# A fused attention and hard-swish kernel: first pair's load converted in the transfer, transpositions, staircases and second bias sums moved

## The chip, the cores and the metric

The kernel runs on one core of one Trainium2 chip. The metric is the device time of one execution in microseconds (us), the median of several runs. A core has five engines that run side by side and wait for each other by semaphores. PE (TensorE) does matrix products and transpositions, DVE (VectorE) elementwise work and scans, ACT (ScalarE) exponentials and copies, POOL (GpSimd) further elementwise work, and SP (SyncE) only issues transfers. POOL issues transfers as well, into a queue of its own; the profile calls it the software queue (q0), and that of SP the hardware queue (q1). A transfer that POOL issues can convert f32 to f16 on the way, and in this kernel only POOL's do.

## What is computed

`q, k, v` are 8 batches of 8 heads of 576 positions of 64 numbers, `s` has one number for each head and position. The output is 4608 rows (batch and position) of 512.

```python
scores = q @ k.T / 8
cum = cumsum(max(s, 0))                        # along the positions of a head
scores = where(causal, -1e9, scores + min(-(cum_i - cum_j), 0))
attn = softmax(scores)                         # sum + 1e-9 below
x = (attn @ v), heads side by side             # 4608 x 512
h = x @ w_in                                   # 512 x 2048
out = (h * clip(h + 3, 0, 6) / 6) @ w_out      # 2048 x 512
```

## The kernel before

**Slots.** The 64 heads are taken in 32 pairs. The main loop (line 718) runs over the pairs p, and one pass through it is called slot p here. Slots 0 to 3 hold attention alone. From slot 4 on, pieces of the second half are laid between the pieces of attention: each `group()` (line 533) emits one piece, either `m1` (four 512-column matmuls `ph` on line 452 for one of 16 column blocks of `h`, then ACT's ReLU on line 467 and DVE's product `gT` on line 468) or `m2` (four matmuls `po` on line 479). A hand-written plan (line 506) says which one comes in slots 4 to 13; later the two alternate as their inputs come ready. After the last slot a tail of `group()` calls works off the rest. All engines take their instructions strictly in the order in which this Python text emits them.

**Attention of a pair.** `load_qk(p, i)` loads q (i = 0) or k (i = 1). For pairs 1 to 10 POOL's queue does it and converts to f16, into a tile `tok` with 96 partitions that hold six positions each. For the pairs for which `flat(p)` is true (p = 0, and p from 11 on) SP or ACT load the f32 numbers into `raw`, and `cast_qk` converts them, on ACT for pair 0 and on POOL later. `transpose_in` puts q or k through PE into a PSUM tile `pt`; `transpose_out` copies `pt` into the tile `qk` on DVE or ACT (`order`, line 211, for the flat form; line 251 for the other). From pair 11 on a transposing transfer (`crossbar_qk`, line 266) and DVE's `spread` take PE's place. `scores` (lines 298 to 335) makes three score tiles of a head in PSUM, each with an exponential on ACT, `corner` the small rest; the score tiles have two buffers. `av` (line 386) multiplies by v, `norm` (lines 408 and 409, DVE) divides by the row sums and makes `x`. `transpose_x` (PE line 423, DVE copy on line 428) puts `x` into `xT`, the input of `m1`; from pair 7 to pair 30 a transposing transfer on SP's queue, `crossbar_x` (line 436), does that.

**The bias.** `cum1` to `cum6` (lines 637 to 665) take the running sums of `s` for 32 heads at a time and split them into rows that the score matmuls can add up. Pair 0 reads them through `pick`. For all later pairs `load_aug` (line 143) copies four rows for each head into partitions 64 to 67 of `qk`; it needs finished rows, and partitions 64 to 127 that nobody writes afterwards. The first 32 heads are done ahead of the loop by DVE and ACT. The second 32, needed from pair 16 on, are done between slots 9 and 13, by POOL except for the scan (line 645), which is DVE's.

**Staircases.** From pair 8 on the causal mask comes from constant staircases in partitions 68 to 127 of `qk`. `set_stair` (line 594) copies them once into each of the four `qk` buffers, a copy for each head: on POOL in slots 6 and 7, on ACT in slots 8 and 9, both heads in one go at the slot's top. `load_aug(p + 2)` has to come behind it, since the copy covers its four partitions too.

**Queues that matter for the change.** ACT's order at the start is: loads, `spos`, `rows_of` (line 690), the two casts of pair 0 (line 183), the two copies of q (line 211). DVE's is: sums (lines 645 to 665), `pick(0)` (line 668), the two copies of k, `pick(1)`. SP's is: `s`, q of pair 0, v of pair 0, then `load_aug(1)` (line 143), which waits for the finished rows, and behind it v of pair 1. POOL's is: constants, q and k of pairs 1 and 2, `cast_v(0)`, q and k of pair 3, `cast_v(1)`, which waits for v of pair 1, and then a long row of loads that ends with the weights `w_in` and `w_out`.

Of the kernel before, what the change touches and what calls it, by code (L numbers as in the profile page):

```python
# [18 lines left out]
def kernel(  # L19
# [10 lines left out]
    nc = tc.nc  # L30
# [7 lines left out]
    NP = NHEADS // 2  # L38
# [5 lines left out]
    NPE = 2 * PPB + 3  # L44
# [4 lines left out]
    NVRAW = 2  # L49
    VW = 66  # L50
    NROW = 1
    NWARM = (16, 4)

# [47 lines left out]
    toks = {}  # L103

    def flat(p):
        return p < 1 or p >= NPE

    def load_qk(p, i, eng=nc.sync):
        b, h0 = p // PPB, 2 * (p % PPB)
        src = (q, k)[i][b, h0 : h0 + 2]  # L110
        if not flat(p):
            if not i:
                tok = work.tile([128, 24 * D], F16, tag="tok", bufs=4, name="tok")
                toks[p] = tok[0:96].rearrange("p (i h e d) -> p i h e d", i=2, h=2, e=6)
            nc.gpsimd.dma_start(
                out=toks[p][:, i].rearrange("p h e d -> p h (e d)"),
                in_=src.rearrange("h (p e) d -> p h (e d)", e=6),
            )
        else:
            eng.dma_start(  # L120
                out=raws[p % NRAW].rearrange("p (i t d) -> p i t d", i=2, t=9)[:, i],
                in_=src.rearrange("h s d -> (h s) d").rearrange(
                    "(t p) d -> p t d", p=128
                ),
            )
# [40 lines left out]
    def fill(eng, ap, value):  # L166

        word = np.array([value, value], np.float16).view(np.float32)[0]
        eng.memset(ap.bitcast(F32), float(word))
# [8 lines left out]
    def cast_qk(p, copy=nc.gpsimd.tensor_copy):  # L178
        tok = work.tile([128, 24 * D], F16, tag="tok", bufs=4, name="tok")
        toks[p] = tok[:, 0 : 18 * D]  # L180
        for i in range(2):
            c = slice(9 * D * i, 9 * D * (i + 1))
            copy(out=toks[p][:, c], in_=raws[p % NRAW][:, c])  # L183
# [373 lines left out]
    def load_s(n, engs):  # L557
# [3 lines left out]
            eng.dma_start(out=C[n][32 * r : 32 * (r + 1)], in_=heads)  # L561

    load_s(0, (nc.sync, nc.scalar, nc.sync, nc.scalar))
    load_qk(0, 0)
    load_qk(0, 1, nc.scalar)
    nc.scalar.preload_act_table_set("natural_log_exp_and_others")
    load_v(0, nc.sync)
    fill(nc.gpsimd, ident, 0.0)
# [6 lines left out]
        base=0,  # L575
        channel_multiplier=-1,
    )
    fill(nc.gpsimd, shut, 0.0)
    for c in (slice(0, 512), slice(512, 640)):
        w = 128 if c.start == 0 else 64  # L580
# [8 lines left out]
            channel_multiplier=-1,  # L589
        )  # L590

    def set_stair(i, copy):
        for hh in range(2):
            copy(
                out=qks[i][64:128, hh, :, 64 * hh : 64 * hh + 640].rearrange(
                    "p i (t c) -> p i t c", c=128
                ),
                in_=stair_sb[64:128, :, None, :].to_broadcast([64, 2, 5, 128]),
            )
# [15 lines left out]
    nc.vector.memset(bias3, 3.0)  # L615
    fill(nc.gpsimd, rows_of[0][:, 0, :], 1.0)
    fill(nc.gpsimd, rows_of[0][:, 1, SEQ:640], 0.0)
    fill(nc.gpsimd, qks[0][64:68, :, :, :], 0.0)
    for i in range(2):
        load_qk(1, i)  # L620
    for i in range(NQK):
# [11 lines left out]
        op=ALU.add,  # L633
    )
    nc.vector.tensor_scalar_mul(out=ident2, in0=ident, scalar1=2.0)

    def cum1(n, eng):
        C["p"] = work.tile([128, SEQ], F32, tag="spos", bufs=1, name="spos")
# [4 lines left out]
    def cum2(n):  # L643
        C["c"] = work.tile([128, SEQ], F32, tag="c8", bufs=1, name="c8")
        nc.vector.tensor_tensor_scan(
            out=C["c"], data0=one.to_broadcast([128, SEQ]), data1=C["p"], initial=0.0, op0=ALU.mult, op1=ALU.add
        )
# [39 lines left out]
        out=C["p"][:, 304:SEQ], in_=C[0][:, 304:SEQ], func=AF.Relu, scale=8.0  # L687
    )
    cum2(0)
    nc.scalar.copy(out=rows_of[0][0:32, 0, 0:SEQ], in_=C["c"][0:32])  # L690
    cast_qk(0, nc.scalar.copy)
    cum3(0, V)
    cum4(0, V)
    cum5(0, V)
    cum6(0, V)
    pick(0)
    transpose(0, 0, (nc.scalar.copy,) * 2)
    transpose(0, 1)
    warm(NWARM[1])
    for g in range(1, 2 * NROW):  # L700
        pick(g)
# [16 lines left out]
    for p in range(NP):  # L718
        nxt = p + 1 < NP
        if NPE <= p + 3 < NP:  # L720
            for i in range(2):
                load_qk(p + 3, i)
        def qk_ahead():
            if PPB < p + 3 < NPE:
                for i in range(2):
                    load_qk(p + 3, i)

        if p == 1:
            load_aug(4, nc.gpsimd)
        elif p == 2:  # L730
            load_w_in(0)
            cast_v(2)
            qk_ahead()
            load_aug(5, nc.gpsimd)
        elif p == 3:
            cast_v(3)
            load_w_in(1)
            qk_ahead()
            load_aug(6, nc.gpsimd)
            cast_v(4)  # L740
        elif p:
            qk_ahead()
            if NPE <= p + 2 < NP:
                cast_qk(p + 2)
                crossbar_qk(p + 2)
            for fn, c in {
                4: ((I, 2),),
                5: ((I, 3),),
                6: ((U, 0), (U, 1), (U, 2), (U, 3)),
                7: ((U, 4), (U, 5), (U, 6), (U, 7)),  # L750
            }.get(p, ()):
                fn(c)
            if nxt:
                cast_v(p + 1)
            if p in (6, 7):
                set_stair((p + 2) % NQK, nc.gpsimd.tensor_copy)
            elif p in (8, 9):
                set_stair((p + 2) % NQK, nc.scalar.copy)
            if p == 4:
                load_aug(7, nc.gpsimd)  # L760
            elif 5 < p < NP - 2:
                load_aug(p + 2, nc.gpsimd)
        if p and p + 2 < NP:
            load_v(p + 2, nc.sync)
        if p == 2:
            nc.sync.dma_start(out=stair_sb, in_=stair_dram.ap())
        if p == 9:
            load_s(1, (nc.sync,) * 4)
            fill(nc.gpsimd, rows_of[1][:, 0, :], 1.0)
        if p == 10:  # L770
            cum1(1, nc.gpsimd)
        if p == 11:
            cum2(1)
            nc.gpsimd.tensor_copy(out=rows_of[1][0:32, 0, 0:SEQ], in_=C["c"][0:32])
        if p == 12:
            cum3(1, nc.gpsimd)
            cum4(1, nc.gpsimd)
        if p == 13:
            cum5(1, nc.gpsimd)
            cum6(1, nc.gpsimd)  # L780

        if p == NPROD + 1:
            x_done[0] = NPROD

        def get(i):
            if p + 1 < NPE:
                transpose(p + 1, i)
            elif nxt:
                spread(p + 1, i)

        if p < PPB:
            scores(p, 0, 0)
            scores(p, 0, 1)
            get(0)
            scores(p, 0, 2)
            corner(p)
            if p:
                av(p - 1, 1, 0)
                av(p - 1, 1, 1)
                norm(p - 1, 1)  # L800
            get(1)
            scores(p, 1, 0)
            scores(p, 1, 1)
            av(p, 0, 0)
            scores(p, 1, 2)
            if p:
                transpose_x(p - 1)
            av(p, 0, 1)
            norm(p, 0)
            continue  # L810

        if p == PPB:
            early[0] = False
            scores(p, 0, 0)
            av(p - 1, 1, 0)
            av(p - 1, 1, 1)
            norm(p - 1, 1)
            m1_begin(0, 0, NKC - 1)
            scores(p, 0, 1)
            transpose_x(p - 1)  # L820
            m1_begin(0, 1, NKC - 1)
            pt = transpose_in(p + 1, 0)
            transpose_out(p + 1, 0, pt, pars=(0,))
            group()
            transpose_out(p + 1, 0, pt, pars=(1,))
            scores(p, 0, 2)
            group()
        else:
            if p == NPROD:
                nc.vector.tensor_scalar(  # L830
                    out=masks, in0=shut, scalar1=65504.0, scalar2=None, op0=ALU.add
                )
            scores(p, 0, 0)
            get(0)
            group()
            scores(p, 0, 1)
            av(p - 1, 1, 0)
            if p >= NPE - 1:
                get(1)
            group()  # L840
            scores(p, 0, 2)
            av(p - 1, 1, 1)
            norm(p - 1, 1)
            group()
        corner(p)
        group()
        if p > NPE:
            x_done[0] = p - 1
        if p == PPB:
            get(1)  # L850
            av(p, 0, 0)
        scores(p, 1, 0)
        if PPB < p < NPROD:
            get(1)
        group()
        if NPROD <= p < NPE - 1:
            get(1)
        scores(p, 1, 1)
        if p != PPB:
            av(p, 0, 0)  # L860
        if PPB < p < NPROD:
            transpose_x(p - 1)
        elif p >= NPROD:
            crossbar_x(p - 1)
        group()
        scores(p, 1, 2)
        group()
        av(p, 0, 1)
        norm(p, 0)
        group()  # L870
# [3 lines left out]
    group()  # L874
    av(p, 1, 1)
    norm(p, 1)
    group()
    group()
    transpose_x(p)
# [31 lines left out]
```

## Time and profile before

| what | value |
|---|---|
| median of 7 runs (lowest to highest) | 360.26 us (358.77 to 362.24) |
| the profiled execution's own time | 362.24 us |
| its span, first to last instruction | 360.5 us |
| mean granted TensorE clock | 0.993 |
| busy share of PE, DVE, ACT, POOL | 96%, 70%, 62%, 35% |
| DMA busy share, 18 to 66 us | 1.15 to 1.19 in four windows |
| DMA busy share from 290 us on | 0.15 or less, except at the very end |

The profile shows one execution, the slowest of the seven that are listed. 1.74 us of its time lie outside its span. A DMA share over 1 is possible because packets on one DMA engine overlap. Matmul ends are modelled, so PE's busy share does not tell how densely its matmuls follow one another; for that the start times are read. Four 512-column matmuls in a row start 0.86 us before the next instruction in nearly all of the trace, eight of `av` 0.25 us, a transposition about 0.05 us.

### The profile page before, as it was taken

The numbers are of one execution on the slowest core, as the hardware profiler recorded it, in microseconds if no ns is written. First come the engines' busy times: TensorE is split into PE (matmuls) and PEld (weight loads), VectorE is DVE, ScalarE is ACT, GpSimd is POOL, SyncE is SP. The second block draws the span as 40 slices with busy tenths as digits, with TensorE's granted clock in tenths as the row PEclk, the third lists the DMA queues.
The fourth block names the chain that finished last, engine by engine and source line by source line (L and its number), as shares of the span: only waits on it lengthen the run. The fifth ranks groups of instructions, "written<-read, shape, count | busy, mean of one in ns | idle before, by whom it ended". The sixth has DMA issues, their size and how long they took to land.

```text
span 360.5 us, 7729 instructions
## 1 busy us (share of the span) xinstructions
PE 347.3 (96%) x2920; PEld 192.0 (53%) x2920; DVE 250.8 (70%) x541; ACT 224.6 (62%) x390; POOL 127.5 (35%) x219
## 2 busy tenths in 40 slices
PE   6999998699999999999999999999999999999995
PEld 2775665455555555555555555555555444444442
DVE  7897996668999867776868677877765544545531
ACT  4987897667677666666666666666665334433310
POOL 7484967654764442425233424343000000000000
PEclk9999999989999999999999999999999999999999
DMA  9899999789999996999897959999321101101111
GB/s 170 149 181 208 169 190 201 166 192 202 163 191 170 230 176 155 191 175 192 156 181 184 199 132 211 153 211 154 79 76 21 58 2 58 58 2 59 58 58 63
DMA packets 146991, 50.88 MB, mean 141 GB/s; under 512 B 133624, under 2 KB 141992, under 8 KB 146952
## 3 DMA queue, kind: packets, MB, share of 16 engines
q1 hardware_dynamic: 135304, 42.13, 58.7%
q0 software_dynamic: 10240, 7.67, 13.9%
q10 hardware_dynamic: 1408, 0.57, 0.7%
q8 instruction: 23, 0.38, 0.5%
q14 instruction: 16, 0.13, 0.1%
HBM read 37.36 MB, written 9.44 MB: 130 GB/s over the span
## 4 chain that ended last, share of the span: by engine, by line
PE 84%; DMA 9%; DVE 3%; POOL 1%; ACT 1%; issue 1%; SPq 0%; POOLq 0%
PE po L479 32%; PE ph L452 31%; PE O L386 7%; PE S L316 6%; DMA w_out_sb<-in_moe_w_out_dram 6%; PE S L305 3%; DMA raw<-in_q_dram 1%; DMA xT<-x 1%; DVE x L409 1%; PE pt L234 1%; PE ptx L423 1%; PE S L298 1%; DVE qk L211 1%; PE Sc L357 0%; POOL w_out_sb L159 0%
## 5 line engine op out<-in xcount | busy, mean ns | idle before, releaser
L468 DVE SCALAR_TENSOR_TENSOR gT<-tr,ph 128x512 f16<-128x512 f32 x144 | 98.9, 687 | 79.8 <-ACT tr L467 78.5
L452 PE MATMUL ph<-xT,w_in_sb 128*128 128x512 f16 x576 | 149.1, 380 | 2.6 <-DMA xT<-x 2.5
L479 PE MATMUL po<-w_out_sb,gT 128*128 128x512 f16 x576 | 146.4, 380 | 0.4 <-DMA w_out_sb<-in_moe_w_out_dram 0.3
L467 ACT ACTIVATE tr<-ph,bias 128x512 f32<-128x512 f32 x144 | 99.0, 688 | 75.6 <-PE ph L452 75.1
L335 ACT ACTIVATE P<-S 128x512 f16<-128x512 f32 x192 | 111.4, 596 | 38.8 <-PE S L305 20.5
L452 PEld LDWEIGHTS <-w_in_sb 128*128 128x128 f16 x576 | 51.9, 98 | 44.9 <-issue 0.9
L479 PEld LDWEIGHTS <-gT 128*128 128x128 f16 x576 | 50.1, 98 | 46.8 <-issue 1.2
L316 PE MATMUL S<-qk 68*128 68x448 f16 (+3 forms) x256 | 49.3, 273 | 1.1 <-ACT P L335 1.1
L386 PE MATMUL O<-va,P 128*128 128x65 f16 x896 | 48.0, 193 | 0.0
L183 POOL CAST tok<-raw 128x576 f16<-128x576 f32 x42 | 28.4, 678 | 54.3 <-DMA raw<-in_q_dram 42.8
L386 PEld LDWEIGHTS <-P 128*128 128x128 f16 x896 | 39.6, 97 | 13.8
L187 POOL CAST va<-vraw 128x512 f16<-128x512 f32 x32 | 20.3, 634 | 61.5 <-DMA vraw<-in_v_dram 48.7
L316 PEld LDWEIGHTS <-qk 68*128 68x128 f16 x256 | 23.9, 99 | 27.8 <-issue 4.6
L143 POOL DMA_DIRECT2D qk<-rows_of x56 | 33.0, 592 | 3.0 <-PE S L305 1.9
L211 DVE COPY qk<-jt 64x768 f16<-64x768 f16 x84 | 32.5, 386 | 1.2
L409 DVE TENSOR_TENSOR x<-O,rl 128x320 f16<-128x320 f32 x64 | 31.5, 492 | 2.2
L495 DVE TENSOR_SCALAR ob<-po 128x512 f32<-128x512 f32 (+1 forms) x36 | 24.4, 678 | 9.8 <-PE po L479 9.2
L337 DVE TENSOR_TENSOR P<-P,shut 128x512 f16<-128x512 f16 x48 | 24.2, 503 | 6.0 <-ACT P L335 5.8
L251 DVE COPY qk<-pt 64x576 f16<-64x576 f16 x30 | 24.1, 803 | 3.1 <-PE pt L234 1.4
L305 PEld LDWEIGHTS <-qk 128*128 128x128 f16 (+1 forms) x256 | 19.0, 98 | 12.5 <-DVE qk L251 0.8
L305 PE MATMUL S<-qk 128*128 128x128 f16 (+1 forms) x256 | 24.9, 219 | 0.1
L386 PE MATMUL O<-va,PC 128*128 128x65 f16 x64 | 12.4, 194 | 0.2 <-DVE PC L369 0.2
(72 smaller groups left out, 172.3 us busy)
## 6 DMA issues: line engine op xcount, KB each, us to landing
out_dram<-ob SPq DMA_DIRECT2D x35, 256.0 KB, 2.0
vraw<-in_v_dram SPq DMA_DIRECT2D x64, 128.0 KB, 3.4
raw<-in_q_dram SPq DMA_DIRECT2D x22, 288.0 KB, 3.9
raw<-in_k_dram SPq DMA_DIRECT2D x21, 288.0 KB, 4.2
w_in_sb<-in_moe_w_in_dram POOLq DMA_DIRECT2D x4, 512.0 KB, 8.3
w_out_sb<-in_moe_w_out_dram POOLq DMA_DIRECT2D x8, 256.0 KB, 9.5
tok<-in_q_dram POOLq DMA_DIRECT2D x10, 144.0 KB, 5.3
tok<-in_k_dram POOLq DMA_DIRECT2D x10, 144.0 KB, 5.3
```

The source lines that it names most:

```text
L143: eng.dma_start(out=qks[p % NQK][64:68, hh, :, 64 * hh : 64 * hh + SEQ], in_=rows_of[g // 32].rearrange("(r g) i t -> g r i t", g=32)[g % ...
L183: copy(out=toks[p][:, c], in_=raws[p % NRAW][:, c])
L211: copies[par](out=qk[0:64, :, i, 128 * par : 128 * par + 256 * n].rearrange("p h (s two c) -> p h s two c", two=2, c=128)[:, :, :, 0, :], ...
L305: mm(S[:, c], lhsT=kT[rows, c], rhs=qT[rows, c], start=(j == 0 and not by_product), stop=(j == 3),)
L316: mm(S[:, c : c + w], lhsT=kT[0:68, 128 * j : 128 * (j + 1)], rhs=qT[0:68, 128 * (j + 1) : SEQ], start=(c == 0), stop=(c != 0 and p >= NROW),)
L335: nc.scalar.activation(out=pt[:, c], in_=S, func=AF.Exp, scale=0.125)
L386: mm(o[:, i, :], lhsT=lhsT, rhs=va[:, hh, j, 0:65], **kw)
L409: nc.vector.tensor_tensor(out=X[p][:, :, hh, :], in0=o[:, :, 0:64], in1=rl.to_broadcast([128, 5, 64]), op=ALU.mult,)
L452: mm(ph, lhsT=w_in_sb[:, kc, ft * 128 : (ft + 1) * 128], rhs=xT[:, kc, n * 512 : (n + 1) * 512], start=(kc == 0), stop=(kc == NKC - 1),)
L467: nc.scalar.activation(out=tr, in_=ph, func=AF.Relu, bias=bias3[:, 0:1])
L468: nc.vector.scalar_tensor_tensor(out=gTs[n][:, ft, :], in0=tr, scalar=6.0, in1=ph, op0=ALU.min, op1=ALU.mult)
L479: mm(po, lhsT=gTs[n][:, ft, t4 * 128 : (t4 + 1) * 128], rhs=w_out_sb[:, ft, :], start=(ft == 0), stop=(ft == NFT - 1),)
```

## The change

There are five parts.

1. Pair 0 is no longer flat. POOL's queue loads its q and k with conversion, right behind the first constant. ACT's casts go; twelve transpositions of 96 columns replace ten of 128, and the copies take the form of line 251: ACT does both of q and one of k, DVE the other of k. On ACT the two copies of q now stand ahead of the `rows_of` copy. The clearing of four partitions of `qk` is split between POOL and DVE. The warm-up matmuls are 12 and 10 instead of 16 and 4.
2. In slots 0 to 3 `transpose_x(p - 1)` comes behind `av(p, 0, 1)` and `norm(p, 0)`.
3. ACT's staircases in slots 8 and 9 are done a head at a time, one behind `corner`, one behind the last scores; `load_aug(10)` and `load_aug(11)` go behind the second.
4. The second bias sums start in slot 12 instead of 9, and everything from the scan on stands in slot 14.
5. After the last slot one more `group()` stands ahead of the last `transpose_x`.

```diff
-    NWARM = (16, 4)
+    NWARM = (12, 10)
...
     def flat(p):
-        return p < 1 or p >= NPE
+        return p >= NPE
...
     load_s(0, (nc.sync, nc.scalar, nc.sync, nc.scalar))
-    load_qk(0, 0)
-    load_qk(0, 1, nc.scalar)
     nc.scalar.preload_act_table_set("natural_log_exp_and_others")
     load_v(0, nc.sync)
     fill(nc.gpsimd, ident, 0.0)
...
+    for i in range(2):
+        load_qk(0, i)
     fill(nc.gpsimd, shut, 0.0)
...
-    def set_stair(i, copy):
-        for hh in range(2):
+    def set_stair(i, copy, heads=(0, 1)):
+        for hh in heads:
...
-    fill(nc.gpsimd, qks[0][64:68, :, :, :], 0.0)
+    fill(nc.gpsimd, qks[0][64:68, 1, :, :], 0.0)
...
     nc.vector.tensor_scalar_mul(out=ident2, in0=ident, scalar1=2.0)
+    fill(nc.vector, qks[0][64:68, 0, :, :], 0.0)
...
     cum2(0)
+    transpose(0, 0, (nc.scalar.copy,) * 2)
     nc.scalar.copy(out=rows_of[0][0:32, 0, 0:SEQ], in_=C["c"][0:32])
-    cast_qk(0, nc.scalar.copy)
     cum3(0, V)
     cum4(0, V)
+    pt = transpose_in(0, 1)
+    transpose_out(0, 1, pt, pars=(0,))
     cum5(0, V)
     cum6(0, V)
     pick(0)
-    transpose(0, 0, (nc.scalar.copy,) * 2)
-    transpose(0, 1)
+    transpose_out(0, 1, pt, pars=(1,))
     warm(NWARM[1])
...
-            elif p in (8, 9):
-                set_stair((p + 2) % NQK, nc.scalar.copy)
             if p == 4:
                 load_aug(7, nc.gpsimd)
-            elif 5 < p < NP - 2:
+            elif p in (6, 7) or 9 < p < NP - 2 and p != 14:
                 load_aug(p + 2, nc.gpsimd)
...
-        if p == 9:
+        if p == 12:
             load_s(1, (nc.sync,) * 4)
             fill(nc.gpsimd, rows_of[1][:, 0, :], 1.0)
-        if p == 10:
+        if p == 13:
             cum1(1, nc.gpsimd)
-        if p == 11:
+        if p == 14:
             cum2(1)
             nc.gpsimd.tensor_copy(out=rows_of[1][0:32, 0, 0:SEQ], in_=C["c"][0:32])
-        if p == 12:
             cum3(1, nc.gpsimd)
             cum4(1, nc.gpsimd)
-        if p == 13:
             cum5(1, nc.gpsimd)
             cum6(1, nc.gpsimd)
+            load_aug(16, nc.gpsimd)
...
             scores(p, 1, 2)
+            av(p, 0, 1)
+            norm(p, 0)
             if p:
                 transpose_x(p - 1)
-            av(p, 0, 1)
-            norm(p, 0)
             continue
...
         corner(p)
+        if p in (8, 9):
+            set_stair((p + 2) % NQK, nc.scalar.copy, (0,))
         group()
...
         scores(p, 1, 2)
         group()
+        if p in (8, 9):
+            set_stair((p + 2) % NQK, nc.scalar.copy, (1,))
+            load_aug(p + 2, nc.gpsimd)
         av(p, 0, 1)
...
     av(p, 1, 1)
     norm(p, 1)
+    group()
     group()
     group()
     transpose_x(p)
```

## The prediction

> **What bounds the kernel now.** I read the page first, then the table of busy time by stretch, then the chain of waits and the timeline where the table shows PE short.
>
> ```profile
> PE 347.3 (96%) x2920; PEld 192.0 (53%) x2920; DVE 250.8 (70%) x541; ACT 224.6 (62%) x390; POOL 127.5 (35%) x219
> ```
>
> PE is the bound on average. By stretches (the columns are start and end, length, then busy us of PE, PEld, DVE, ACT and POOL, granted clock, DMA share, GB/s):
>
> ```profile
> 54.00:66.00 12.00, 10.95 (x109) 6.45 (x108) 8.11 (x16) 8.89 (x14) 8.50 (x13) 1.00 1.18 197
> 66.00:72.00 6.00, 3.10 (x36) 1.91 (x35) 3.76 (x7) 4.26 (x7) 3.65 (x7) 1.00 0.63 156
> 72.00:76.00 4.00, 4.00 (x25) 2.04 (x23) 2.06 (x4) 1.54 (x4) 1.33 (x2) 0.57 1.14 220
> 76.00:88.00 12.00, 12.00 (x117) 7.09 (x116) 9.04 (x21) 10.25 (x20) 6.01 (x8) 1.00 0.85 183
> ```
>
> PE is full from 76 us on, so there only what PE loses can be won. Before, it is short at 54 to 72, and at 72 to 76 its clock is 0.57. The chain of waits says why:
>
> ```profile
> 57.65 8.64 DMA w_out_sb<-in_moe_w_out_dram
> ...
> 66.33 0.26 PE po L479
> 66.59 4.37 DMA xT<-x
> ...
> 71.00 0.38 PE ph L452
> ...
> 73.89 1.71 PE ph L452 x4
> ```
>
> The last `w_out` lands at 66.29 and PE starts at 66.33; then PE waits for `xT` until 71.00. The row `ph` x4 at 73.89 takes 1.71 instead of 0.86: half clock after the wait. Added over the rows from 71.84 to 75.71, the slow clock costs about 1.66 us (1.24 for 0.86, 0.43 for 0.22, 0.39 for 0.22, 1.71 for 0.86, 0.11 for 0.06). So **two bounds stand in line: the loads until 71 us, then PE.** An edit ahead of 66 us counts only if it moves the loads; behind 76 us, only if PE loses there today.
>
> **Part 1, the start.** It removes two ACT casts (1.24 us together) and two raw loads, and adds two POOL issues (0.81 and 0.68) behind the constant that ends at 1.24.
>
> ```profile
> DMA to landing us min/median/max: 3.6/4.2/4.7
> ```
>
> That is `tok` before 12 us, issue to landing. So q should land at 4.9 to 6.0 (raw q today: 6.98), k 0.7 later. Then six transpositions (about 0.4 with the way to ACT), ACT's two copies (0.65 start to start) and the `rows_of` copy (0.67): rows ready on ACT at 7.3 to 8.4. DVE's sums end at 8.59 today and do not move: they start when `s` lands, 4.12, and the added DVE clearing (768 words; 256 words took 0.27, so 0.8) fits between 3.07 and 3.87. Thus DVE stays the later one, `pick(0)` runs 8.62 to 9.0, and its one copy of k takes 0.81 where two took 1.01 (9.02 to 10.03). First scores: some 0.15 us earlier, no more.
>
> PE's start is worth nothing by itself, since 66.29 comes from the loads. What counts is when POOL's row of loads starts: POOL stands idle 4.54 us until 15.44 for v of pair 1. SP issues that at 10.08, behind `load_aug(1)`, behind the rows at 8.59: unmoved. But POOL waits 0.73 today at 8.84 for v of pair 0, which stood behind raw q on SP's queue; without this wait `tok` of pair 3 is issued up to 0.7 earlier and leaves the engines free sooner for v of pair 1. The DMA share is 0.67 at 14 to 18 and 1.15 to 1.19 from 18 to 66, so an earlier start is an earlier end. Gain between 0 and 0.7; I take 0.4. The other end: ACT's rows get late once q lands after 6.1; at the page's median for `tok`, 5.3, it lands at 6.6, 0.5 late. Range -0.5 to 0.7. POOL's second pair is issued 0.75 later (two issues more, half of a 1.44 us clearing less) and lands near 9.8 and 10.5; PE wants it at 10.7 and 11.6.
>
> The Trainium skill ("DMA: Bandwidth & Descriptors", section "Issuing engine by pattern") gives simple loads to Sync and calls that path generally faster, which speaks against this part. In this trace the raw q on SP's queue took 5.33 us to landing and `tok` 3.6 to 4.7. Were the rule right here, q would land behind 6.98 at best and the rows some 0.9 late, and the sum would be near zero; I follow the row.
>
> **Part 2, transpositions in slots 1 to 3.** PE waits 0.30 us ahead of three of them (0.47 to 0.51 counted start to start), 1.5 us in all. But see DVE there:
>
> ```profile
> 18.60 0.18 DVE L408 RECIPROCAL rl<-O 128x5 f32<-128x5 f32 x1
> 18.82 0.49 DVE L409 TENSOR_TENSOR x<-O,rl 128x320 f16<-128x320 f32 x1
> 19.23 1.62 DVE L251 COPY qk<-pt 64x576 f16<-64x576 f16 x2
> 20.88 0.19 DVE L408 RECIPROCAL rl<-O 128x5 f32<-128x5 f32 x1
> 21.11 0.49 DVE L409 TENSOR_TENSOR x<-O,rl 128x320 f16<-128x320 f32 x1
> 21.63 0.81 DVE L251 COPY qk<-pt 64x576 f16<-64x576 f16 x1
> 22.47 0.46 DVE L428 COPY xT<-ptx 128x576 f16<-128x576 f16 x1
> ```
>
> No bracket for idle time: DVE is full, 4.25 us a slot (the next row of line 408 starts at 22.85), with the same instructions afterwards. Next late is `L305`, which waits for DVE's copy (18.20) today already. I take 0; between 0 and 1.5, and the loads hide even that.
>
> **Part 3, staircases.** Both halves together, and what they hold up:
>
> ```profile
> 57.80 2.41 ACT L594 COPY qk<-stair_sb 64x1280 f16<-64x1280 f16 x2
> ...
> 60.89 0.38 PE L316 MATMUL S<-qk 68*128 68x320 f16 x2 [0.95 <-ACT P L335]
> ...
> 66.68 2.41 ACT L594 COPY qk<-stair_sb 64x1280 f16<-64x1280 f16 x2
> ...
> 71.00 0.38 PE L452 MATMUL ph<-xT,w_in_sb 128*128 128x512 f16 x1 [2.46 <-DMA xT<-x]
> ```
>
> In slot 8 PE stands from 59.78 (its last start at 59.53, eight times 0.03) to 60.89: 1.11 us. In halves that shrinks to little, but PE then comes earlier to `po`, which waits for the `w_out` that land at 62.90 and 66.29, so 0; were the loads earlier by so much, up to 1.11. In slot 9 the copies lie today inside the wait until 71.00 and cost nothing. Afterwards they lie behind it, two bursts of 1.2 us on an ACT that is 85% busy at 76 to 88, and the exponentials behind each come up to 1.2 later, against two score buffers. Cost 0 to 1.11 (as in slot 8); nearer to 0, since each burst is half as long: 0.2.
>
> The move takes POOL along: `load_aug(11)` stands behind ACT's second half of slot 9, and `cast_qk(12)`, `cast_v(11)` and `load_aug(12)` behind it. Today these casts run at 73.79 and 77.37; ACT's second half would end near 82, the two issues take 1.15, so the first lands 2.2 to 5.5 later (median 3.9 in 60 to 130 us): 84 to 87.5, and the scores of slot 11 want it at 87.03. On SP, `crossbar_qk(12)` slips from 80.89 to some 84.6; 4.0 to landing makes 88.6, and DVE's `spread` wants it at 89 to 90.5. It fits with about 1 us to spare. The same delay in slot 8 falls into the time that waits for `xT`.
>
> **Part 4, second sums.** DVE's scan (88.97, 1.35 us) makes PE late twice in slot 11: 0.22 ahead of 92.81 (`gT`), and
>
> ```profile
> 94.27 0.20 PE L386 MATMUL O<-va,PC 128*128 128x65 f16 x1 [0.24 <-DVE PC L369]
> ```
>
> which is 0.41 start to start: 0.63 in all. In slot 14 DVE runs without a pause from 112 to 118 and has its first one, 1.11, at 119.29; the scan may cost the same there or nothing. The plan gives slot 11 six pieces and lays no bound on slot 14, so a slot is longer (9 us instead of 8) for the same DVE work: I take 0.15, a gain of 0.5 (0 to 0.63). POOL's new work there (0.77, 0.83, 0.43, 1.28, 0.67, 1.28 from its rows: 5.3 us, and 2.4 for casts) fits the slot, POOL being 39% busy at 112 to 121, and `load_aug(16)` has all of slot 15 to land.
>
> **Part 5, the tail.** One more piece ahead of
>
> ```profile
> 279.64 0.45 PE L423 MATMUL ptx<-ident,x 128*128 128x128 f16 x5 [0.19 <-DVE x L409]
> ```
>
> The four `ph` at 278.42 are issued by 279.28, so 0.36 is lost; a piece of 0.86 covers it. The pieces are only reordered. Gain 0.36 (0 to 0.36).
>
> **Sum.** 0.4 + 0 - 0.2 + 0.5 + 0.36 = about 1.05 us. Against the profiled execution: 362.24 - 1.05 = 361.2. That execution is 1.98 above the median, and its slow clock (1.66) may well be missing in others, so I lay the sum on the median: 360.26 - 1.05 = **359.2 us**. By the unknowns' ends this case runs from 358.4 to 360.0.
>
> **Rivals.** (a) *The loads give way.* Everything that PE loses before 71 us comes back: 0.7 from the loads, 1.11 from slot 8, 0.63 and 0.36, 2.8 in all: 357.5; if the clock stays up as well, 355.8. For it speak PE's visible waits; against it, that the `w_out` issues on POOL follow landings one by one (waits of about 1 us each), so transfers and not PE set their pace. (b) *Nothing moves but the tail*: the start is hidden, the scan's 0.63 goes along to slot 14: 359.9, or 360.3 if slot 9 eats it. (c) *POOL's queue turns slower.* `load_aug(11)` or `jt` of pair 12 misses slot 11. It decides from a landing over 5 us on; each us late is a us of PE. Late by 2.5, as `xT` is in slot 9, it gives 360.26 - 1.05 + 2.5 = 361.7, and with 1.66 for the clock, as there, 363.4; I put it at 362.5.
>
> The Trainium skill ("TensorE: Matmul & The Clock Gate", section "Part 1: The HAM clock gate (the "warmup" mystery)") has the clock fall after an idle window of about 3.4 us. Here it fell after a wait of 2.46. By the rule (c) would end at 361.7; the row says that 363.4 is possible.
>
> **Numbers.** My forecast 0.37, (a) 0.33, (b) 0.17, (c) 0.13. A difference of 0.5% (1.8 us: 358.46 and 362.06) is about what a measurement of this kernel can tell from none. Forecast and (b) lie within it: 0.54 same. (a) lies below: 0.33 faster. (c): 0.13 slower. The range takes in most of (a) and the near part of (c): 356.9 to 361.8.
>
> **What would show it.** Right: the first `L305` near 9.8, POOL's `cast_v(1)` at 14.7 to 15.4, the last `w_out` and the `xT` that ends PE's long wait earlier by the same amount; DVE still without idle in slots 1 to 3; no wait at the last `transpose_x`; slot 11 free of the two waits. Wrong: `rows_of` on ACT later than DVE's last sum; a wait of `L305` for `load_aug` in slot 11; the wait for `xT` shorter by over 1 us, or gone; a wait ahead of `L452` or `L386` in slot 14.

## The result, and the profile after

| | median of its runs (lowest to highest) | ratio to before, 95% interval |
|---|---|---|
| before | 359.98 us (358.60 to 362.44, 38 runs) | 1 |
| after | 364.47 us (360.48 to 366.67, 16 runs) | 1.0081 [1.0056, 1.0106] |

The change makes the kernel slower. The time of after stands at levels: 360.5, 362, 363.5, 365.5 and 366.5 us. The intervals leave out executions more than 1.5% above the lowest of their kernel, so the ratio is nearer to 1 than that of the medians (1.0125). The profiled execution shown here took 366.45 us (span 364.7), a high one; that of before, 362.24, was one of the highest of its kernel too.

PE's busy time and two costly groups of the page of after:

```profile
PE 350.6 (96%) x2924; PEld 193.5 (53%) x2924; DVE 254.7 (70%) x541; ACT 224.4 (62%) x389; POOL 129.0 (35%) x221
L452 PE MATMUL ph<-xT,w_in_sb 128*128 128x512 f16 x576 | 149.0, 380 | 5.2 <-DVE gT L468 2.6
L143 POOL DMA_DIRECT2D qk<-rows_of x56 | 33.1, 593 | 17.4 <-ACT qk L594 15.0
```

The shares are those of before and say nothing. The last column does: PE's `ph` stood 2.6 us for DVE's `gT`, and POOL stood 15.0 us for ACT's staircases, ahead of `load_aug`. Before, POOL stood there for 3.0 us in all:

```profile
L143 POOL DMA_DIRECT2D qk<-rows_of x56 | 33.0, 592 | 3.0 <-PE S L305 1.9
```

The stretches after (columns as in the prediction):

```profile
66.00:72.00 6.00, 3.42 (x36) 1.93 (x36) 5.20 (x8) 3.39 (x5) 2.91 (x5) 0.94 0.89 178
72.00:76.00 4.00, 4.00 (x26) 2.13 (x25) 1.93 (x5) 1.48 (x4) 0.00 (x0) 0.66 1.13 237
76.00:88.00 12.00, 8.28 (x79) 4.70 (x78) 9.08 (x13) 9.55 (x16) 6.00 (x10) 1.00 0.55 92
88.00:92.00 4.00, 4.00 (x21) 1.95 (x20) 2.63 (x8) 1.53 (x3) 1.91 (x4) 0.57 0.60 130
```

The first two are as before: the wait for `xT`, then slow clock. The third is new. PE was full there before and is now busy 8.28 of 12, and in the fourth its clock is 0.57 a second time. These are PE's waits in it:

```profile
80.31 0.40 PE L305 MATMUL S<-qk 128*128 128x128 f16 x4 [0.82 <-ACT P L335]
84.52 0.38 PE L305 MATMUL S<-qk 128*128 128x128 f16 x4 [0.17 <-ACT P L335]
87.52 1.09 PE L452 MATMUL ph<-xT,w_in_sb 128*128 128x512 f16 x4 [2.62 <-DVE gT L468]
```

The chain of waits of after tells where the last one comes from:

```profile
80.90 1.25 ACT qk L594
...
82.81 1.85 DVE P L337
84.66 1.78 DVE qk L211
...
87.52 1.09 PE ph L452 x4
```

ACT's second half of slot 9 ends at 82.15. It releases POOL, whose timeline shows it:

```profile
82.45 0.57 POOL L143 DMA_DIRECT2D qk<-rows_of  x1 [4.23 <-ACT qk L594]
83.02 1.28 POOL L183 CAST tok<-raw 128x576 f16<-128x576 f32 x2
```

ACT then does one exponential, which releases DVE's `L337` (a minimum of two f16 tiles). The two `spread` copies follow it (`L211`). Before and after:

```profile
81.48 0.42 DVE L337 TENSOR_TENSOR P<-P,shut 128x512 f16<-128x512 f16 x1
81.81 0.65 DVE L211 COPY qk<-jt 64x768 f16<-64x768 f16 x2
```

```profile
82.81 1.85 DVE L337 TENSOR_TENSOR P<-P,shut 128x512 f16<-128x512 f16 x1 [0.58 <-ACT P L335]
84.59 2.17 DVE L211 COPY qk<-jt 64x768 f16<-64x768 f16 x2
```

POOL's casts, which begin 0.21 us behind the start of `L337`, run beside the minimum and the first copy until 85.37; from 85.32 POOL issues transfers. By these two rows `gT` is 2.9 us late, and PE waits for it.

### The profile page after: what moved, and what is told of

It is laid out like the page before. It is cut to its first block, busy times and chain, and to the rows that moved or that the text cites. A ratio compares the mean times of both kernels' runs of the same rounds, so it can differ in the third digit from the quotient of the medians.

```text
span 364.7 us, 7733 instructions
## 1 busy us (share of the span) xinstructions
PE 350.6 (96%) x2924; PEld 193.5 (53%) x2924; DVE 254.7 (70%) x541; ACT 224.4 (62%) x389; POOL 129.0 (35%) x221
## 4 chain that ended last, share of the span: by engine, by line
PE 82%; DMA 6%; DVE 6%; ACT 3%; issue 1%; POOL 1%; ACTq 0%; DVEq 0%; POOLq 0%
PE po L479 33%; PE ph L452 30%; PE S L316 7%; PE O L386 7%; DMA w_out_sb<-in_moe_w_out_dram 5%; PE S L305 3%; ACT P L335 2%; DVE qk L251 1%; DMA xT<-x 1%; PE pt L234 1%; DVE gT L468 1%; DVE qk L211 1%; ACT tr L467 1%; DVE P L337 1%; PE Sc L357 0%
## 5 line engine op out<-in xcount | busy, mean ns | idle before, releaser
L452 PE MATMUL ph<-xT,w_in_sb 128*128 128x512 f16 x576 | 149.0, 380 | 5.2 <-DVE gT L468 2.6
L452 PEld LDWEIGHTS <-w_in_sb 128*128 128x128 f16 x576 | 52.0, 98 | 47.4 <-issue 3.7
L187 POOL CAST va<-vraw 128x512 f16<-128x512 f32 x32 | 21.1, 660 | 55.8 <-DMA vraw<-in_v_dram 46.4
L211 DVE COPY qk<-jt 64x768 f16<-64x768 f16 x84 | 32.0, 381 | 1.2
L337 DVE TENSOR_TENSOR P<-P,shut 128x512 f16<-128x512 f16 x48 | 25.5, 531 | 5.5 <-ACT P L335 5.4
L251 DVE COPY qk<-pt 64x576 f16<-64x576 f16 x31 | 24.9, 803 | 3.3 <-PE pt L234 1.6
L305 PEld LDWEIGHTS <-qk 128*128 128x128 f16 (+1 forms) x256 | 18.9, 97 | 14.8 <-DVE qk L251 3.1
L305 PE MATMUL S<-qk 128*128 128x128 f16 (+1 forms) x256 | 24.8, 219 | 2.0 <-ACT P L335 1.0
L408 DVE RECIPROCAL rl<-O 128x5 f32<-128x5 f32 x64 | 11.9, 186 | 0.9 <-PE O L386 0.5
```

What stands on the lines that cost most here:

```text
L211: copies[par](out=qk[0:64, :, i, 128 * par : 128 * par + 256 * n].rearrange("p h (s two c) -> p h s two c", two=2, c=128)[:, :, :, 0, :], ...
L305: mm(S[:, c], lhsT=kT[rows, c], rhs=qT[rows, c], start=(j == 0 and not by_product), stop=(j == 3),)
L337: nc.vector.tensor_tensor(out=pt[:, c], in0=pt[:, c], in1=masks[:, c], op=ALU.min)
L452: mm(ph, lhsT=w_in_sb[:, kc, ft * 128 : (ft + 1) * 128], rhs=xT[:, kc, n * 512 : (n + 1) * 512], start=(kc == 0), stop=(kc == NKC - 1),)
```

## The theories

Start to start, PE's losses in slots 8 to 11 of after were 2.62 (`xT`), 0.98, 0.34 and 2.79 us. What is to blame? **Q**: the hold of POOL's queue puts its casts onto DVE's operations. **A**: ACT's two bursts as such. **S**: the new start, whose first `L305` is 0.77 us later. **L**: the loads set the pace up to 71 us, so the start is absorbed. **P**: wherever POOL computes longer, DVE and PE lose. **N**: the parts do not depend on each other. Every experiment is given with the median of its own runs; before had a median of 359.64 to 359.91 in the four sets.

## Experiments

**1. Which part.** `stairs_back` is after without part 3, `stairs_only` before with part 3 alone:

```diff
# stairs_back: after with
+            elif p in (8, 9):
+                set_stair((p + 2) % NQK, nc.scalar.copy)
...
-            elif p in (6, 7) or 9 < p < NP - 2 and p != 14:
+            elif 5 < p < NP - 2 and p != 14:
...
-        if p in (8, 9):
-            set_stair((p + 2) % NQK, nc.scalar.copy, (0,))
...
-        if p in (8, 9):
-            set_stair((p + 2) % NQK, nc.scalar.copy, (1,))
-            load_aug(p + 2, nc.gpsimd)
```

> The changed kernel with part 3 undone: ACT's staircases of slots 8 and 9 at the slot's top again, both heads at once, load_aug(10) and (11) back in POOL's row. Theory Q (POOL's queue, held behind ACT's second half, pushes POOL's casts into the time of DVE's copies, DVE falls behind, PE waits about 2.8 us at 87 us and loses clock after it): the time falls from about 362.9 to 359 to 360.3, ratio to before 0.997 to 1.001; POOL's idle time ahead of load_aug (17 us in the changed kernel) goes back to 3, no PE wait over 1 us behind 76 us. Theory S (the start: rows 0.6 us later, first scores 0.8 us later): stays at 362 to 363. Theory A (ACT's two bursts themselves make PE wait): as Q here.

> The kernel before with part 3 alone. Q and A: slower than before by 2 to 3.5 us, ratio 1.005 to 1.010, with the PE wait for DVE's gT at 85 to 90 us. S: no difference, ratio 0.998 to 1.002.

Measured: `stairs_back` 358.41 us, ratio 0.9983 [0.9957, 1.0009]; `stairs_only` 361.94, 1.0069 [1.0045, 1.0093]. Part 3 makes the loss, by itself too, as both Q and A expected; without it the time is even below the range that was given. `stairs_only` had no wait for `xT` in its profile and still lost 1.82 and 1.67 us ahead of `L452`, both times for `gT`.

**2. The start.** `start_back` is after with part 1 undone (warm-ups, loads, casts and transpositions as before). `start_only` was meant to be before with part 1 alone, but the kernel that ran under this name has none of part 1. It differs from before in two lines, which change nothing of what it does:

```diff
# start_back: after with
-    NWARM = (12, 10)
+    NWARM = (16, 4)
...
-        return p >= NPE
+        return p < 1 or p >= NPE
...
# start_only: before with
-    def set_stair(i, copy):
-        for hh in range(2):
+    def set_stair(i, copy, heads=(0, 1)):
+        for hh in heads:
```

> The changed kernel with part 1 undone: q and k of pair 0 by SP and ACT in f32 and cast by ACT, warm-up 16 and 4. S: falls by 2 us or more, to 360 to 361. Q and A: stays within 1 us of the changed kernel, 362 to 363.5; the first scores back at 9.95 us, the wait at 87 us still there.

> The kernel before with part 1 alone (q and k of pair 0 converted in the transfer). The prediction: 0.4 us faster, ratio 0.998 to 1.000. Theory S (the start costs: rows 0.6 us later, first scores 0.8 us later): 0.5 to 1 us slower, ratio 1.0015 to 1.003. Theory L (the loads of 18 to 66 us take up either): ratio 0.999 to 1.001, the last w_out lands within 0.3 us of 66.29.

Measured: `start_back` 364.29 us, 1.0119 [1.0079, 1.0158]; `start_only` 359.61, 0.9997 [0.9979, 1.0015]. S expected `start_back` at 360 to 361, and it stayed with after (364.47): the start is not what makes the loss. In `start_back` the first `L305` stands at 9.93, as before, and the two waits for `gT` remain, 1.46 and 2.78 start to start. `start_only` is the kernel before once more. It shows how closely that kernel repeats, and gives a second profile of it; on part 1, and on L, it says nothing. No run has part 1 alone.

**3. Parts 4 and 5, and part 2.** `sums_tail_only` is before with the second sums and the extra piece in the tail, `transposes_only` before with part 2.

```diff
# transposes_only: before with
-            if p:
-                transpose_x(p - 1)
             av(p, 0, 1)
             norm(p, 0)
+            if p:
+                transpose_x(p - 1)
             continue
```

> The kernel before with parts 4 and 5 alone (second bias sums in slots 12 to 14, one more piece ahead of the last transpose_x). The prediction's terms: 0.5 + 0.36 = 0.86 us faster, ratio 0.9965 to 0.9985, no wait at 92 to 95 us and none at the last transpose_x. Rival: the scan's wait moves along to slot 14: 0.36 faster, ratio 0.9985 to 0.9995, a wait of 0.4 to 0.7 us near 112 to 120.

> Before with part 2 alone. The prediction's step (DVE is full in slots 1 to 3, so the waits of PE only move): ratio 0.999 to 1.001, DVE still 4.25 us a slot. The rival (PE bounds there): 1.5 us faster, 0.996.

Measured: 357.83 us, 0.9955 [0.9932, 0.9978], and 359.77, 1.0001 [0.9982, 1.0019]. The sums gain 1.85 together with the tail, more than twice what was forecast. The profile of `start_only`, the kernel before with its scan in slot 11, shows the larger part of it:

```profile
91.33 0.20 PE L386 MATMUL O<-va,PC 128*128 128x65 f16 x1 [1.09 <-DVE PC L369]
```

This wait (1.26 us start to start) was 0.41 in the profiled execution of before, whose PE was already late from `xT`. `transposes_only` has it too (1.33), and so has `pool_busy` of experiment 5 (1.42).

**4. The halves without the hold.** `stairs_unheld` is after, but `load_aug(10)` and `load_aug(11)` are issued behind the casts of slots 9 and 10:

```diff
             set_stair((p + 2) % NQK, nc.scalar.copy, (1,))
-            load_aug(p + 2, nc.gpsimd)
...
+            if p in (9, 10):
+                load_aug(p + 1, nc.gpsimd)
```

> The changed kernel with ACT's staircases in halves as they are, but load_aug(10) and (11) issued a slot later, behind the casts, so that POOL does not stand still for ACT. Q: POOL's casts of pair 12 go back to about 74 us, DVE's min and spread in slot 10 take 0.4 and 0.35 us instead of 1.85, no PE wait over 1.2 us at 80 to 90; 359.3 to 360.8, ratio 0.998 to 1.002. A: PE still waits 2 us or more at 80 to 90, 362 to 363. S: 362 to 363 without that wait.

Measured: 357.53 us, 0.9959 [0.9926, 0.9993], below what any theory gave. Its profile keeps ACT's 0.98 and 0.34, and the 2.79 is gone. DVE there:

```profile
77.94 0.42 DVE L337 TENSOR_TENSOR P<-P,shut 128x512 f16<-128x512 f16 x1 [0.58 <-ACT P L335]
78.28 0.65 DVE L211 COPY qk<-jt 64x768 f16<-64x768 f16 x2
```

The bursts are all there, so A does not explain the loss. With this, `stairs_quarters` cut the staircases into four parts:

```diff
+            stair_part((p + 2) % NQK, nc.scalar.copy, 0, 1)
...
+            stair_part((p + 2) % NQK, nc.scalar.copy, 1, 0)
```

> The changed kernel with load_aug(10) and (11) issued a slot later, as in the version that lets POOL run, and ACT's staircases cut into four parts of a slot instead of two. If the two PE waits for ACT that are left there (0.98 and 0.34 us) come from the length of the bursts: 0.5 to 1 us below that version, 356.5 to 357.2, ratio 0.991 to 0.995. If they come from ACT's total work: no change, 357.5.

Measured: 362.71 us, 1.0025 [0.9989, 1.0062]. This failed. Its profile has five waits of 0.33 to 0.81 instead of two, only two of them for ACT. But the profiled execution is its fastest (358.11 us); ten of the twelve took 360.79 to 364.52, and no trace shows what they waited for.

**5. POOL's computing by itself.** `pool_busy` is before with four more casts a slot on POOL in slots 16 to 25, into a tile that nobody reads:

```diff
+            if 16 <= p < 26:
+                for _ in range(4):
+                    nc.gpsimd.tensor_copy(out=spare, in_=C["c"])
```

> The kernel before with four more POOL casts (f32 to f16, 128x576, of a tile that stands still, into a spare tile that nobody reads) at the top of slots 16 to 25; all outputs as before. Theory P (DVE operations that read two SBUF inputs or copy SBUF to SBUF wait while POOL computes, those that read PSUM do not): in 130 to 222 us the mean of DVE's min (line 337) and spread (line 211) goes up by half or more, single ones to 1 us and over, lines 409, 468 and 495 stay at 0.49, 0.69 and 0.69; the time goes up by 0 to 3 us. Rival N (no coupling; DVE was late for its inputs): all of DVE's durations stay, the time too.

Measured: 359.70 us, 1.0004 [0.9979, 1.0028]. P as a cause of lost time falls, though DVE did stretch. Groups of DVE at 130 to 222 us (busy us, mean ns of one, idle before), `pool_busy` (its lines are one further down) and then before:

```profile
L469 DVE SCALAR_TENSOR_TENSOR gT<-tr,ph 128x512 f16<-128x512 f32 x40 | 27.3, 683 | 13.3 <-ACT tr L468 12.9
L212 DVE COPY qk<-jt 64x768 f16<-64x768 f16 x20 | 12.3, 618 | 0.3
```

```profile
L468 DVE SCALAR_TENSOR_TENSOR gT<-tr,ph 128x512 f16<-128x512 f32 x40 | 27.5, 688 | 21.3 <-ACT tr L467 20.9
L211 DVE COPY qk<-jt 64x768 f16<-64x768 f16 x20 | 7.2, 360 | 0.3
```

The copy from SBUF to SBUF went from 360 to 618 ns, and DVE's idle time ahead of `gT` paid for it (21.3 to 13.3). `gT`, which reads PSUM, kept its duration. The minimum's mean went up less than P said, from 474 to 539 ns. Here DVE had idle time to give, and the collisions cost nothing.

**6. The two holds, and the hold without bursts.** `hold9_only` frees slot 8's hold and keeps slot 9's. `hold_only` is `sums_tail_only` with whole staircases, where POOL's casts of slots 9 and 10 wait for the slot's first exponential. `unheld_sums_tail` is before with parts 4 and 5 and unheld halves.

```diff
# hold9_only: after with
-            load_aug(p + 2, nc.gpsimd)
+            if p == 9:
+                load_aug(p + 2, nc.gpsimd)
...
# hold_only: sums_tail_only with
...
+            if p in (9, 10):
+                nc.scalar.copy(out=tick, in_=ident[:, 0:2])
+                nc.gpsimd.tensor_copy(out=tock, in_=tick)
+                cast_qk(p + 2)
+                crossbar_qk(p + 2)
+                cast_v(p + 1)
```

> After, with only slot 8's hold taken away: load_aug(10) goes behind slot 9's casts, load_aug(11) stays behind ACT's second half in slot 9. Theory Q, by the two waits in the trace: the second hold (2.79 us of PE and the slow clock) stays and the first (0.98) goes: 361.5 to 363.5. If the first hold is what matters: 357.5 to 358.5.

> Before with parts 4 and 5, staircases at the slot's top as before; in slots 9 and 10 POOL's casts of pairs 11 and 12 are made to wait for the slot's first exponential on ACT (by a two-column copy on ACT that one on POOL reads). No staircase is split and no load of rows is held. Theory Q (casts held back on POOL fall on DVE's SBUF operations): slower than the 357.83 of the kernel with parts 4 and 5 alone by 1.5 to 3 us, 359.3 to 360.8, with DVE's L338 or L212 over 1 us each and PE waiting for gT in slots 9 to 11. Theory A (ACT's two bursts are what costs): no change, 357.5 to 358.3.

> Before with parts 4 and 5 and with ACT's staircases in halves, the rows' loads behind the next slot's casts; neither part 1 nor part 2. If the first pair's and the transpositions' moves are worth nothing, as the run with part 1 alone says, this equals the kernel after with unheld staircases (357.5) within 0.7 us, 356.8 to 358.2. If the earlier weights of part 1 are what the unheld halves live on, it is slower: 358.5 or more. If the wait for xT comes back in some executions, they stand at 361 to 363.

Measured: `hold9_only` 364.55 us, 1.0103 [1.0068, 1.0139]; `hold_only` 357.88, 0.9947 [0.9931, 0.9964]; `unheld_sums_tail` 360.88, 0.9990 [0.9958, 1.0022]. So the second hold carries the loss, though the time lies above the 361.5 to 363.5 expected, and 0.88 of the first wait, which was to go, is still in the profile. `unheld_sums_tail`, whose expectation counts on `start_only` for part 1, missed its 356.8 to 358.2: three of its twelve executions are there (357.33 to 357.57), nine are not, while `stairs_unheld`, which adds parts 1 and 2, has eight of twelve at 357.71 or less. So N is not shown, and whether parts 1 and 2 make the slower executions rarer stays open. And `hold_only` (five executions) cost nothing, so Q as it stood failed. In slot 10 of its profile the casts start 0.5 us *ahead* of the minimum, which then takes 0.43. In all seven places where ACT's half held POOL (two each in after, `stairs_only`, `start_back`, one in `hold9_only`) they start 0.211 to 0.213 us *behind* it, and it takes 1.843 to 1.851. Released by neighbours in ACT's queue, the two kept their distance in all seven. Q became: the hold fixes the phase, and the phase decides.

**7. The phase.** `hold_phase` is `sums_tail_only` with the hold of the change, released by a copy of two columns on ACT in the place of the second half; no bursts. `hold_shifted` keeps bursts and hold, but a two-column copy on POOL takes the wait and `load_aug` follows the casts, which so come 0.6 us earlier.

```diff
# hold_phase: sums_tail_only with
...
+        if p in (8, 9):
+            nc.scalar.copy(
+                out=qks[(p + 2) % NQK][64:128, 1, :, 64:66],
+                in_=stair_sb[64:128, :, 0:2],
+            )
+            load_aug(p + 2, nc.gpsimd)
...
# hold_shifted: stairs_unheld with
...
+            nc.gpsimd.tensor_copy(
+                out=tock[64:128], in_=qks[(p + 2) % NQK][64:128, 1, 0, 64:66]
+            )
```

> Before with parts 4 and 5, ACT's staircases whole at the slot's top; in slots 8 and 9 load_aug(10) and load_aug(11) stand where the change has them, behind a copy of ACT of two columns (0.2 us) in the place of the second half. So POOL's casts stand behind ACT in the order of the change, without its bursts of 1.25 us. Theory Q in its present form (the release by ACT sets POOL's casts 0.21 us behind the start of DVE's L337, which then takes 1.85 us): L337 at 1.8 us in slots 9 and 10, PE waits for gT there, 359.5 to 362.5. Theory A (ACT's bursts are needed): 357.5 to 358.5, as with parts 4 and 5 alone.

> After, with ACT's halves and POOL's hold at the same place, but a copy of two columns on POOL waits for the half, and load_aug(10), load_aug(11) follow behind the casts of slots 9 and 10 (0.57 us of issue less ahead of the casts). Theory Q in its present form: the casts now start ahead of DVE's L337, which takes 0.93 at most, and PE's waits of 2.5 to 2.8 us for gT go: 357.5 to 360. Theory A, or the hold as such: 363 to 365, as after.

Measured: `hold_phase` 359.48 us, 0.9994 [0.9974, 1.0014], against 357.83 without the hold: at the lower end of what Q gave and above what A gave. No burst, and in slot 10 of its profile the collision is back (POOL, DVE, then PE):

```profile
78.00 1.28 POOL L183 CAST tok<-raw 128x576 f16<-128x576 f32 x2
```

```profile
78.19 1.45 DVE L337 TENSOR_TENSOR P<-P,shut 128x512 f16<-128x512 f16 x1
79.56 2.01 DVE L211 COPY qk<-jt 64x768 f16<-64x768 f16 x2
```

```profile
82.34 1.02 PE L452 MATMUL ph<-xT,w_in_sb 128*128 128x512 f16 x4 [1.94 <-DVE gT L468]
```

In slot 9 the hold did not meet the minimum (0.42). `hold_shifted` took 360.57 us, 1.0000 [0.9968, 1.0032], between the ranges of Q and A. In its profile (358.65 us, one of the lower executions) the casts start 0.28 us ahead of `L338`, which takes 0.66, and PE's waits for `gT` shrink from 2.79 to 0.50, 0.86 and 0.37. Five of its twelve executions took 358.06 to 358.83, seven 360.41 to 364.75. What the seven slower ones waited for is not traced. The phase changes the size of the first collision, but what exactly decides is not shown: in `hold_phase` the cast starts 0.19 ahead and still runs the minimum to 1.45. The hold also sets up the later one with `spread` (1.43 us for two in `hold_shifted`), which shifting does not remove. And casts are not all that holds `spread`: the next pair of copies in `hold_shifted` ran beside nothing but four issues of transfers on POOL, and one copy of the two took 1.23:

```profile
80.80 1.53 DVE L212 COPY qk<-jt 64x768 f16<-64x768 f16 x2
```

```profile
80.15 2.28 POOL L144 DMA_DIRECT2D qk<-rows_of  x4
```

## Why the prediction was wrong

**The step that failed** is part 3's move of POOL: "It fits with about 1 us to spare". It asked when transfers would land and followed the queue to `load_aug(11)` and `jt`. They did arrive: no wait of `L305` for `load_aug`, and none in slot 11. It priced the casts at nothing because their results came in time, and never asked what runs *beside* them at their new place. They fell on DVE's minimum and `spread`, with DVE the releaser of PE's next `ph`. Rival (c) gave slower 13 chances in 100, and its price (2.5 us, with 1.66 for the clock) was close, but its mechanism, a late transfer, was not the one that happened. The page on the GPSIMD of the Trainium skill ("GPSIMD Engine Reference", section "8. Key points") has GpSimd share its SBUF interfaces with VectorE, with contention for instructions with two SBUF inputs or in a two-port mode. The traces agree for the minimum, which has two (`L337` 0.42 to 1.85); whether `spread`, which has one, runs in such a mode, no run shows. A reading of that page beside the moved casts would have named the rival.

**The size.** By the levels, the hold of slot 9 costs 4.0: the profiled execution of `hold9_only`, which has no long wait for `xT`, took 361.24, `stairs_unheld` mostly about 357.3. Of this 2.54 is the wait in its profile, and the slow clock behind it makes most of the rest: the granted clock is 0.66 over 83 to 88 us, which is 1.7 us of full speed. In `hold_phase`, idle for 1.94 ahead of the same line, the clock stayed 1.00. Two executions of after took 360.48 and 360.56 at a mean clock of 0.999; there the clock did not fall, and the hold cost about 3.2. The ends that the prediction gave for its own case do not follow from its terms either: these add up to 358.6 and 361.9, not to 358.4 and 360.0. After lies beyond both.

**The base.** "Two bounds stand in line: the loads until 71 us, then PE" was read from an execution that is not the usual one. All five profiled executions that show the long wait for `xT` (before, after, `stairs_back`, `sums_tail_only`, `unheld_sums_tail`) are in the upper group of their kernel, and the eleven others show at most 0.2 there. In the five the last `w_out` landed at 65.78 to 67.13, in the eleven at 62.83 to 65.03. Before and `start_only`, which do the same work:

```profile
30.00:42.00 12.00, 11.56 (x130) 7.38 (x128) 10.88 (x18) 11.11 (x22) 8.83 (x17) 1.00 1.19 195
```

```profile
30.00:42.00 12.00, 11.56 (x131) 7.37 (x128) 10.88 (x18) 11.10 (x22) 9.05 (x15) 1.00 1.27 214
```

The loads moved 195 GB/s in one and 214 in the other; the last `w_out` landed at 66.29 and 63.32, and in the second `xT` arrives as it is wanted. The profiled executions with the wait stand above the medians of their kernels by 2.3 (before), 3.0 (`sums_tail_only`) and 4.1 (`stairs_back`). With 357.5 and 4.0 this gives 363.8 to 365.6, about the median of after; it is a sum of levels, not a measurement. It does not explain everything: four executions of `hold9_only` took 364.52 to 364.85 at the same mean clock as its two lower ones (0.994 to 0.995), so no second fall of the clock is behind their 3.3, and what is was not traced. What sets the rate of the loads stays open, and so does how often the wait comes: 3 of 12 executions of `sums_tail_only` stand over 1.5 us above its lowest, 4 of 12 of `stairs_unheld`, 9 of 12 of `unheld_sums_tail`, but one of the 3 and three of the 9 at a mean clock of 1.0, where no slow clock followed. That most executions of after have the wait is read from their times and clocks, not from traces of each.

**Part 1** was forecast at 0.4, and no run measures it by itself. Its mechanism did not come. The q of pair 0 landed at 5.71, inside the forecast, and k at 7.08, but DVE's sums, said not to move, ended at 9.20 instead of 8.59: `spos` took 0.81 instead of 0.44 and `L662` 0.75 instead of 0.46. The first `L305` came at 10.72, not near 9.8. POOL's row of loads began later, not earlier: `cast_v(1)` stands at 15.37 to 16.91 in the six traces with part 1, and at 14.56 to 15.44 in the ten without. The last `w_out` landed at 66.08 and 66.29 in after and before, and what a later row costs is not shown. That PE's start is worth nothing by itself fits `start_back`, whose first scores are 0.79 earlier and whose time is that of after, in a spread of 5 to 6 us.

**Part 2** was right at 0, by its reason: DVE is full with 4.25 us a slot before, and in after its `L408` rows stand at 21.57 and 25.83, 4.26 apart. PE's waits at `L423` fell by 0.2 and came back ahead of `L305`.

**Part 3's ACT term** was forecast as a loss of 0.2. In the profiles the halves are a gain: waits of 1.11, 0.42, 0.34 and 0.80, as `start_only` shows them in slots 8 and 9, give way to 0.98 and 0.34. The times do not settle it: the medians of `stairs_unheld` and `stairs_back` are 0.9 apart (357.53 and 358.41) with overlapping intervals, and `unheld_sums_tail` is slower than `sums_tail_only` (360.88 and 357.83), although its lowest executions are 0.4 faster. The forecast let the loads hide slot 8, which holds for the execution it read.

**Part 4** was right in its place and too small: the scan costs 1.26 to 1.42 in slot 11 where PE is not late from `xT`, not 0.63, and nothing in slot 14. **Part 5**: the wait at the last `transpose_x` is gone, as forecast.

## What to carry to other kernels

When a step is moved behind another engine's work, follow its queue to what runs beside it, not only to what waits for it: check which instructions slow each other at its new time, and whether the slowed engine releases the bound. A moved wait that hangs on a neighbour of another release can fix the distance between the two, so that a collision comes back each time, as in the seven places here. And read a base from more than one execution: a wait that comes and goes (here `xT`) moves the price of everything near it. The kernel without part 3 is 358.41, not clear of before; before with parts 4 and 5 alone, 357.83, and after with unheld halves, 357.53, beat both kernels, and of these two `sums_tail_only` is the steadier (no execution above 360.8).

## What the runs showed of the hardware

- DVE's f16 operations from SBUF to SBUF stretch when POOL computes: `L337` 0.42 to at most 1.85 us, two `spread` copies 0.65 to 2.17, while those reading PSUM (`gT` 0.69, `x` 0.49) keep their time. Over the sixteen traces from 30 us on, 312 minima that overlap a computing instruction of POOL took 0.40 to 1.85 us, and 456 that overlap none at most 0.43; the 738 `gT` that overlap one took at most 0.69.
- Issues of transfers on POOL alone left the minimum alone (103 of them, at most 0.43), but not always `spread`: one copy took 1.23 us beside them.
- What decides whether the minimum or the cast waits is open. Three casts that began 0.211 to 0.213 us behind the minimum's start held it to 1.85 in seven of seven places. The same order 0.228 us behind (`unheld_sums_tail`, at 122.05 us) left it at 0.42, and so did a cast of v 0.210 us behind (`stairs_quarters`, at 60.15 us).
- PE's clock fell around the end of each of the eight waits of 2.25 us and more (idle 2.25 to 2.87) and stayed up behind those of 1.94 and less.
